# Loading and rounding a second weight piece ahead of x, and making the first scores in two halves, at the start of a fused attention and feed-forward kernel

## The chip, the cores and the metric

The kernel runs on one core of a Trainium2 chip. The metric is device time in microseconds (us) of that core. A run is one execution; most comparisons below rest on 5 runs of each kernel, taken in turn with runs of the kernel before on the same chip.

Names: TensorE multiplies matrices (PE in the profile, PEld for its weight loads), VectorE is DVE, ScalarE is ACT, SP issues the transfers.

## The reference, cut to what matters

```python
# x (8, 8, 512, 64), state (8, 8, 32, 64): batches, heads, tokens or states, width
scores = scale * x @ state.T           # softmax over the 32 states, for each token
xread  = softmax(scores) @ state
scores2 = scale * state @ x.T          # softmax over the 512 tokens, for each state
sread  = softmax(scores2) @ x
h = concat(xread, sread) @ w_in        # 4352 tokens x 512, w_in 512 x 2048
out = gelu_quick(h) @ w_out            # w_out 2048 x 512
```

The weights arrive as 64-bit floating-point words and are rounded to 32 bits on the chip, in pieces of 128 rows by 512 columns (512 KB each).

## The kernel before

It doesn't compute xread. It first multiplies the state by w_in (the product M) and then the softmax by M (h). So the first useful h matmul needs two things: four rounded pieces of w_in, from which M is made, and the normalised, transposed softmax of batch 0 (`aT`). All of this happens in the first 31 us, for which this is the code (comments are mine):

```python
def keep_warm(n):                         # warming: matmuls of zeros, 0.22 us each in the traces
    ps = psH.tile([P, FC], FP32, tag="h", name="warm")
    for _ in range(n):
        nc.tensor.matmul(ps, zeros[:, :P], zeros, start=True, stop=True)

def round_a(i):                           # a piece, first part: mask on VectorE, two passes on ScalarE
    ...
    nc.vector.tensor_scalar(sc, hi, 0x7FF00000, None, ALU.bitwise_and)
    ...
    nc.scalar.activation(out=sc.bitcast(FP32), in_=sc, func=AF.Relu, bias=edge[0], scale=-8.0)
    nc.scalar.activation(out=sc, in_=sc.bitcast(FP32), func=AF.Relu, bias=edge[1], scale=-1.0)

def round_b(i):                           # second part: four operations on VectorE
    nc.vector.tensor_scalar(fr, hi, 0xFFFFF, 0x100000, ...)
    nc.vector.scalar_tensor_tensor(sc, hi, -0x80000000, sc, ...)      # needs ScalarE's passes
    nc.vector.scalar_tensor_tensor(dst, lo, 2.0**-32, fr, ...)
    nc.vector.scalar_tensor_tensor(dst, dst, 2.0**-20, sc.bitcast(FP32), ...)

def att_xT_arriving(b, warm):             # x of batch 0, chunk by chunk as it lands
    for c in range(SCH):                  # 4 chunks of 128 tokens
        keep_warm(warm)
        ...                               # four transposes on TensorE
        (nc.scalar.copy if c % 2 else nc.vector.tensor_copy)(A[b]["xT"][...], ps)
...
load_weights(1); load_state(0); load_x(0); load_weights(NPR)     # NPR = 4
load_state(1); load_x(1); load_weights(2 * NPR)
keep_warm(11)
round_to(1, 0)          # piece 0
att_state(0)
att_xT_arriving(0, 2)
att_scores(0)           # all 512 tokens at once
powers_to(2)            # round_a of piece 1
att_blocks(0)           # transposes on VectorE
att_x_exp(0)            # maximum, subtraction, exponential
round_to(2, 1)
att_x_norm(0)           # sum, inverse, product, transpose: aT
keep_warm(24)
att_state(1)
...                     # transposes and scores of batch 1
keep_warm(24)
powers_to(4)
round_to(NPR, 2)        # pieces 2 and 3
att_M(0, 0)             # the first useful product, and its copy on ScalarE
att_blocks(1); att_x_exp(1)
up_x(0, 0) ...          # the first h
```

In the timelines the instructions of one engine stand in this order, and a wait stands with what ended it: VectorE's 1.34 us ahead of 6.91 us, for one, with ScalarE's pass.

## Time and profile before

| | |
|---|---|
| time, 3 runs | 747.86 us median (747.64 to 749.01) |
| span of the profiled run | 745.8 us |
| first M / first h on TensorE | 29.16 us / 31.00 us |
| fourth rounded piece ready on VectorE | 28.90 us |
| VectorE busy, 4.81 to 12.21 us | 4.04 of 7.40 us |
| VectorE busy, 12.21 to 28.90 us | 16.35 of 16.69 us |
| TensorE at half clock | 43.39 to 46.80 us |

TensorE is busy from here to the end (98% of the span), so what counts is when its first useful matmul starts, and whether it is held up or slowed after that. The lines are in the prediction.

### The profile page before, as it was taken

What the parts mean: (1) busy time and instruction counts of PE and PEld (TensorE: products, weight loads), DVE (VectorE), ACT (ScalarE), POOL (GpSimd) and SP (SyncE); (2) the same over time, 40 slices, a digit from 0 to 9 for tenths busy, and PEclk for the clock granted to TensorE, in tenths of its full rate; (3) what the DMA queues carried; (4) which work ended last, traced back from release to release, by engine and by line L of the source; (5) the groups of instructions that cost most, each with busy time, mean ns of one, the idle gap of its engine ahead of it and who ended that gap; (6) DMA issues with size and microseconds to landing.
All of it is one profiled execution on the core that took longest, in us unless ns stands there. A gap on an engine that the chain in (4) does not pass through costs nothing.

```text
span 745.8 us, 10913 instructions
## 1 busy us (share of the span) xinstructions
PE 732.2 (98%) x4553; PEld 568.0 (76%) x4555; DVE 501.9 (67%) x947; ACT 231.6 (31%) x421; POOL 0.8 (0%) x8
## 2 busy tenths in 40 slices
PE   8989999999999999999999999999999999999996
PEld 3423444458788798888888789878888888899995
DVE  5999699705946776576756765677657774768340
ACT  4667610121424411443134421451143313300220
POOL 0000000000000000000000000000000000000000
PEclk9999999999999999999999999999999999999999
DMA  9811246010012000300040003100030001000000
GB/s 234 337 58 56 85 142 173 0 54 3 29 46 45 1 15 30 74 1 15 2 102 1 15 2 83 21 1 16 29 74 1 15 2 42 1 15 29 15 1 28
DMA packets 48768, 35.29 MB, mean 47 GB/s; under 512 B 36432, under 2 KB 44112, under 8 KB 48720
## 3 DMA queue, kind: packets, MB, share of 16 engines
q1 hardware_dynamic: 48720, 34.61, 16.2%
q8 instruction: 35, 0.57, 0.3%
q14 instruction: 13, 0.11, 0.0%
HBM read 25.69 MB, written 8.91 MB: 46 GB/s over the span
## 4 chain that ended last, share of the span: by engine, by line
PE 95%; SPq 2%; DMA 1%; ACT 1%; issue 0%; DVE 0%; DVEq 0%; ACTq 0%
PE o L646 28%; PE o L891 16%; PE o L523 9%; PE h L462 8%; PE o L480 7%; PE low L598 6%; PE upx L891 6%; PE o L598 4%; PE M L280 4%; PE xT L262 2%; SPq L138 1%; PE sr L411 1%; PE o L280 1%; PE upx_sr L891 1%; DMA out_dram<-osb_sr 1%; PE warm L122 1%
## 5 line engine op out<-in xcount | busy, mean ns | idle before, releaser
L901 DVE TENSOR_TENSOR g<-o,g 128x512 f32<-128x512 f32 (+1 forms) x140 | 88.1, 651 | 87.4 <-PE o L891 86.3
L646 PE MATMUL o<-w_out,g 128*128 128x256 f32 x576 | 130.0, 380 | 0.0
L646 PEld LDWEIGHTS o<-w_out,g 128*128 128x128 f32 x576 | 107.4, 190 | 18.1 <-issue 4.2
L898 ACT ACTIVATE g<-g 128x512 f32<-128x512 f32 (+1 forms) x84 | 49.8, 599 | 100.5 <-DVE g L901 100.5
L891 PE MATMUL upx<-aT,M 128*128 128x256 f32 x192 | 49.3, 379 | 0.0
L891 PE MATMUL o<-ta,M 128*128 128x256 f32 x192 | 49.3, 379 | 0.0
L891 PE MATMUL o<-ta,ms 128*128 128x256 f32 x192 | 48.4, 380 | 0.0
L391 ACT COPY M<-M 128x512 f32<-128x512 f32 x64 | 33.2, 596 | 42.3 <-PE M L280 42.3
L646 PE MATMUL o<-sums,g 128*128 128x256 f32 x192 | 43.8, 382 | 0.0
L523 PE MATMUL o<-w_out,g 128*128 128x256 f32 x192 | 42.9, 380 | 0.0
L646 PE MATMUL o<-sums,later 128*128 128x256 f32 x192 | 42.4, 379 | 0.0
L646 PEld LDWEIGHTS o<-sums,g 128*128 128x128 f32 x192 | 35.6, 190 | 8.6 <-issue 4.2
L523 PEld LDWEIGHTS o<-w_out,g 128*128 128x128 f32 x192 | 36.1, 190 | 6.0 <-issue 1.3
L891 PEld LDWEIGHTS o<-ta,ms 128*128 128x128 f32 x192 | 36.4, 190 | 5.2 <-DVE osb L542 0.3
L891 PEld LDWEIGHTS upx<-aT,M 128*128 128x128 f32 x192 | 36.5, 190 | 5.0
L646 PEld LDWEIGHTS o<-sums,later 128*128 128x128 f32 x192 | 36.5, 190 | 5.0
L891 PEld LDWEIGHTS o<-ta,M 128*128 128x128 f32 x192 | 36.5, 190 | 5.0
L503 DVE TENSOR_TENSOR later<-g,g 128x512 f32<-128x512 f32 (+1 forms) x32 | 20.8, 650 | 21.5 <-ACT g L465 21.5
L462 PE MATMUL h<-low,M 128*128 128x512 f32 x64 | 31.5, 630 | 2.1 <-ACT M L391 2.1
L280 PE MATMUL M<-w_in,stT 64*32 64x512 f32 x512 | 33.2, 594 | 0.2 <-ACT eT L401 0.2
L462 PE MATMUL h<-aT,M 128*128 128x512 f32 x64 | 28.7, 599 | 2.3 <-ACT M L391 2.3
L601 DVE TENSOR_TENSOR pu<-low,pu 128x128 f32<-128x128 f32 x12 | 3.5, 291 | 39.6 <-PE low L598 39.6
(172 smaller groups left out, 1135.5 us busy)
## 6 DMA issues: line engine op xcount, KB each, us to landing
later<-in_moe_w_out_dram SPq DMA_DIRECT2D x16, 512.0 KB
xn<-in_x_dram SPq DMA_DIRECT2D x28, 256.0 KB
w_out<-in_moe_w_in_dram SPq DMA_DIRECT2D x12, 512.0 KB
out_dram<-osb SPq DMA_DIRECT2D x20, 256.0 KB
out_dram<-later SPq DMA_DIRECT2D x12, 256.0 KB
later<-in_moe_w_in_dram SPq DMA_DIRECT2D x4, 512.0 KB
sums<-in_x_dram SPq DMA_DIRECT2D x4, 256.0 KB
stn<-in_state_dram SPq DMA_DIRECT2D x16, 32.0 KB
```

The source lines that it names most:

```text
L262: nc.tensor.transpose(ps[:, c], x_heads(b, c, j), ident)
L280: nc.tensor.matmul(ps[g][st], A[b]["stT"][rows, st], rhs(rows, j), start=True, stop=True)
L391: nc.scalar.copy(m[:, g], ps[g])
L462: nc.tensor.matmul(hps, lhs[i], rhs[i], start=(i == 0), stop=(i == n - 1))
L480: nc.tensor.matmul(ops, G[key, f // 2][:, f % 2, P * r : P * (r + 1)], w_out[:, f], start=(f == 0), stop=(f == NF - 1))
L503: nc.vector.tensor_tensor(out=s1, in0=a21, in1=a22, op=ALU.add)
L523: nc.tensor.matmul(ps[:, r], lhs[f][:, P * r : P * (r + 1)], rhs[:, f], start=(first and r == 0 and f == 0), stop=(f == HF - 1), skip_grou ...
L598: nc.tensor.matmul(ps, lhs[f], rhs[:, f], start=(f == 0), stop=(f == QF - 1))
L646: nc.tensor.matmul(ps[:, r], lhs[f][:, P * r : P * (r + 1)], rhs[:, f], start=(r == 0 and f == 0), stop=(f == HF - 1), skip_group_check=True,)
L891: nc.tensor.matmul(ps[:, k], lhs[i][:, o : o + P], rhs[i], start=(first and k == 0 and i == 0), stop=(i == n - 1), skip_group_check=True,)
L898: nc.scalar.activation(out=dst, in_=src, func=AF.Gelu_apprx_sigmoid)
L901: nc.vector.tensor_tensor(out=dst, in0=ps, in1=x, op=ALU.add)
```

## The change

The intent is to use the time in which VectorE waits. The second piece of w_in is loaded ahead of x and rounded while x is still on its way; and the first softmax is begun on the first 256 tokens as soon as these are there. To pay for the late x, all four copies of transposed x go to ScalarE, and fewer warming matmuls stand in front of M. The diff, cut to its core:

```diff
-    def round_a(i):
+    def mask(i):
         ...                                  # the mask alone, so that it can be issued early
+    def round_a(i):
+        if i not in power:
+            mask(i)
@@ att_xT_arriving
-            keep_warm(warm)
+            if c < 2:
+                keep_warm(warm)
 ...
-            (nc.scalar.copy if c % 2 else nc.vector.tensor_copy)(A[b]["xT"][...], ps)
+            nc.scalar.copy(A[b]["xT"][...], ps)
+            if c % 2:
+                att_half(b, c // 2)
+    def att_half(b, i):                      # scores of 256 tokens, their transposes,
+        ...                                  # maximum and subtraction
@@ the start
-    load_weights(1)
+    load_weights(2)
 ...
-    keep_warm(11)
-    round_to(1, 0)
+    keep_warm(16)
+    powers_to(2)
+    round_to(2, 0)
     att_state(0)
     att_xT_arriving(0, 2)
+    nc.scalar.activation(out=A[0]["e1"], in_=A[0]["e1"], func=AF.Exp, scale=scale)
     att_scores(0)
     powers_to(2)
-    att_blocks(0)
-    att_x_exp(0)
-    round_to(2, 1)
+    round_to(3, 0)
     att_x_norm(0)
 ...
     att_scores(1)
-    keep_warm(24)
+    keep_warm(14)
     powers_to(4)
     round_to(NPR, 2)
     att_M(0, 0)
```

The whole scores of batch 0 are still made, because the other softmax needs them. Behind the first M the lists of instructions are the same on every engine.

## The prediction

> **What bounds the kernel now.** I read the page first: matmuls fill the core, and the chain that ended last is almost all TensorE.

> ```profile
> PE 732.2 (98%) x4553; PEld 568.0 (76%) x4555; DVE 501.9 (67%) x947; ACT 231.6 (31%) x421; POOL 0.8 (0%) x8
> PE 95%; SPq 2%; DMA 1%; ACT 1%; issue 0%; DVE 0%; DVEq 0%; ACTq 0%
> ```

> Behind such a queue a saving counts only if real TensorE work starts sooner or an idle time of TensorE goes. "Busy" includes the warming matmuls, which compute nothing, so I next read the chain in order of time over the first 50 us (columns: start, length, what).

> ```profile
> 24.32 4.91 PE warm L122 x22
> 29.23 1.15 PE M L280 x16
> 30.39 0.57 ACT M L391
> 31.00 7.15 PE h L462 x16
> ...
> 41.51 0.48 ACT M L391
> ...
> 42.03 8.84 PE h L462 x16
> ```

> The useful stream starts with the first product M, at 29.16 us in the timeline; from there to the end TensorE hardly rests. So the change is worth what it takes off 29.16. M needs two things: the end of the warming queue, and four rounded pieces of w_in from VectorE. The timeline of VectorE shows that both come nearly together.

> ```profile
> 4.81 0.43 DVE L189 TENSOR_SCALAR low<-w_out 128x512 int32<-128x512 int32 x1 [3.68 <-DMA w_out<-in_moe_w_in_dram]
> ...
> 6.91 0.69 DVE L205 SCALAR_TENSOR_TENSOR low<-w_out,low 128x512 int32<-128x512 int32 x1 [1.34 <-ACT low L195]
> ...
> 9.95 0.69 DVE L273 COPY xT<-xT 128x512 f32<-128x512 f32 x1 [0.42 <-PE xT L272]
> 12.21 0.43 DVE L189 TENSOR_SCALAR low<-w_out 128x512 int32<-128x512 int32 x1 [1.56 <-DMA w_out<-in_moe_w_in_dram]
> ...
> 28.21 0.69 DVE L207 SCALAR_TENSOR_TENSOR w_in<-w_in,low 128x512 f32<-128x512 f32 x1
> ```

> The fourth piece is done at 28.90, 0.26 us before M. From 12.21 VectorE has no named wait; before that it waits 3.3 us in three places. Thus VectorE is the real bound of the start, and the 24 warming matmuls in front of M only fill its time. A table of stretches confirms this and shows one more thing, the clock.

> ```profile
> core 0: us, PE busy (x) PEld busy (x) DVE busy (x) ACT busy (x) POOL busy (x), PEclk, DMA share, GB/s
> 4.81:12.21 7.40, 6.17 (x44) 2.83 (x42) 4.04 (x8) 2.77 (x5) 0.00 (x0) 1.00 1.11 284
> 12.21:28.90 16.69, 16.21 (x95) 7.67 (x89) 16.35 (x27) 10.57 (x16) 0.00 (x0) 1.00 1.03 331
> 43.39:46.80 3.41, 3.41 (x5) 1.35 (x4) 3.34 (x7) 1.93 (x3) 0.00 (x0) 0.50 0.00 0
> ```

> VectorE is busy 4.04 of 7.40 us in the first stretch and 16.35 of 16.69 in the second. In the last one, TensorE ran at half clock for 3.41 us although it was fully busy: half of that, 1.7 us, is lost on the bounding engine (16 h matmuls took 8.84 us instead of 7.15).

> [...] the half-clock stretch is 3.41 us, and just before it TensorE idles 2.12 us (39.91 to 42.03) waiting for the copy of M. [...] that window, 39.97 to 43.39, still had about 40% of work. [...] 5.0 to 8.5 us, where all packets are under 512 B (x), moved 237 GB/s; stretches of weights alone, from 24 us on, move about 400.

> **The change, part by part.** The order of instructions on each engine, which the built kernel shows, differs in the start alone; behind the first M all engines have the same lists.

> *Transfers.* The second piece (512 KB) goes ahead of x. At 400 GB/s it lands 1.3 us behind the first, at an estimated 6.1 us instead of 12.2, and x arrives up to 1.3 us later. Bytes up to the third piece are the same, so all else arrives as before.

> *VectorE.* Mask of piece 0 at 4.81; mask of piece 1 at 6.1, inside the wait for ScalarE that ends at 6.91 as before; the remaining three operations of piece 0 until 8.85; four of piece 1, 0.34+0.60+0.72+0.69 = 2.35 us by their spacing in the timeline, until 11.2. The first half of the scores should be there: chunk 1 of x, transposed at 7.96 before, comes about 9.0-9.2; its copy on ScalarE (0.59) ends near 10.3; the half scores take an estimated 0.6 (1.09 for whole ones); 11.0. Each half costs VectorE two transposes of 256 columns (estimate from 655 ns at 512 and 1245 at 1024: 0.36 each), a maximum and a subtraction of 512 (0.69 each): 2.1 us, so 13.2. The second half of x, copied by ScalarE one chunk after the other, gives scores about 13.4, so VectorE ends the second half at 15.4. Then a new wait: the third piece is masked only now, and ScalarE does the exponential (1.06) first and its two passes for the piece (0.72 each) after it: they end about 17.9, while VectorE has only 0.75 us of its own. I put the wait at 1.8 us. Three operations (2.0): 19.9. Normalising as before (1.24+0.22+0.38+1.26+1.2 = 4.3): 24.2. Three masks and one mask of the fraction (1.4), a wait of 0.45 for ScalarE's passes on the fourth piece, three operations (2.05): 28.15.

> As a ledger: gone are the waits of 0.42 and 1.56 and two copies of 0.69, 3.36 us; new are waits of about 0.2, 1.8 and 0.45 and 0.2 for the smaller operations, 2.65. VectorE gains about 0.7 us, 28.90 to 28.2.

> *TensorE.* Whole scores of batch 0 are still made for the other softmax, so 16 matmuls of half width are added twice, about 1.1 us, all in the start. Warming matmuls go from 11+8+24+8+24 = 75 to 16+4+24+8+14 = 66. From the second half scores (12.7): 0.6 for these, 1.02 for the whole scores, 24 warming matmuls at 0.216 (5.2): 19.5; four transposed groups at 0.87 with 0.1 ahead (3.6) 23.1, x of batch 1 has long landed; scores of batch 1 as before, 1.8 from the last transpose: 24.9; 14 warming matmuls and the small gap 3.3: 28.2. The shorter warming queue was evidently cut to meet VectorE at the same moment.

> *Sum.* M starts at 28.2-28.3 instead of 29.16: 0.9 us. Everything behind it keeps its order. ScalarE ends its passes for pieces 4 and 5 at about 29.0, and M's product needs it at 29.4, so the 0.9 survives; the idle time before 42.03 moves along with it, because it consists of ScalarE's queue behind the last gelu (four passes, two copies).

> **The rivals.** (1) *The half-clock window.* [...] the same 2.12 us of idle may be split between two windows and the 1.7 us loss goes. With the phase of the recorded run, the idle would lie at 39.0 to 41.1, about 1.0 and 1.1 us in two windows, neither half idle: 745.2 us. For it: the shift alone would do it. Against it: the phase may be new in every run; then the chance of a loss is the same before and after. All three times of before and the profiled run are 747.6 or more, so the loss seems common there. (2) *New waits eat the gain*: x or the copies, now all on ScalarE, arrive a microsecond later than I put them, the second half and the exponential follow, and M starts at 29.2 again: 747.8. For it: four copies in series on one engine and a late x. Against it: the warming queue of 14 suggests an earlier M. (3) *The start loses its clock.* With no warming between the later chunks TensorE may idle enough to be halved; the 24 warming matmuls then take up to 1.7 us more and M slips: 748.5. For it: over a microsecond of waits lies between 9 and 13 us. Against it: windows there were 80% busy before and no loss came.

> **Range and chances.** 747.86 - 0.9 = 746.9 with the half-clock loss in the middle run; 745.2 without. I weigh these about three to two and take a little off for the second: 746.4. The range is 744.9 (both gains, and 0.3 more) to 747.9 (no gain). 2% is 15 us, while the whole start before M is 29 us and its bound moves by one: within 2% 0.99, faster 0.01, slower 0.

> **What would show it.** In the profile of the changed kernel: the first M near 28.2, VectorE's fourth piece ending just before it, a wait of about 1.8 us of VectorE for ScalarE's pass near 16-18 us, no wait for the second piece, scores half done near 11.0. The clock of 39 to 47 us tells whether the 1.7 us came back. I'm wrong if M starts at 28.2 and the time does not fall by 0.9 at an equal number of half-clock stretches, or if M waits for VectorE past 28.6.

## The result, and the profile after

The changed kernel took 745.72 us in the median of 4 runs (745.65 to 747.58), the kernel before 747.75 with one more run. Ratios here are the mean time of one kernel's runs over that of the other's of the same rounds, so not quite the ratio of the quoted medians: it was 0.9978, with a 95% interval of 0.9956 to 1.0. The time lies in the predicted range and below the predicted 746.4. But the four runs are three at 745.65 to 745.77 and one at 747.58, and nothing in between.

The page of the changed kernel, first the engines, then the chain:

```profile
PE 730.2 (98%) x4576; PEld 567.4 (76%) x4578; DVE 501.1 (67%) x949; ACT 232.7 (31%) x423; POOL 0.8 (0%) x8
PE 96%; DMA 2%; ACT 1%; SPq 0%; issue 0%; DVE 0%; DVEq 0%; ACTq 0%
```

TensorE was busy 2.0 us less, 730.2 instead of 732.2, although it has 23 more matmuls. Something took less time for each matmul. The chain in order of time (start, length, what) shows where it went:

```profile
25.88 2.75 PE warm L122 x12
28.63 1.55 PE M L289 x16
30.18 0.57 ACT M L415
...
30.80 7.15 PE h L486 x16
...
41.30 0.48 ACT M L415
...
41.82 7.15 PE h L486 x16
```

The first h starts at 30.80; before, it was 31.00. This is all that the start has won: 0.2 us, where I had reckoned 0.9. The second group of 16 h starts 0.2 us earlier as well, at 41.82, but takes 7.15 us where before it took 8.84. That is the other 1.7 us. The table of stretches has the clock (columns as in the prediction; the sixth after the length, the number ahead of the DMA share, is the granted clock):

```profile
4.81:12.21 7.40, 6.31 (x43) 2.95 (x42) 5.79 (x12) 4.14 (x7) 0.00 (x0) 1.00 1.04 251
12.21:28.90 16.69, 15.86 (x120) 7.57 (x125) 13.79 (x24) 9.43 (x15) 0.00 (x0) 1.00 0.99 308
37.53:40.95 3.42, 2.17 (x17) 0.31 (x16) 3.39 (x5) 2.92 (x5) 0.00 (x0) 1.00 0.00 0
40.95:44.36 3.41, 2.54 (x6) 1.25 (x7) 3.34 (x7) 1.82 (x5) 0.00 (x0) 1.00 0.03 7
```

VectorE does 1.75 us more in the first stretch (5.79 against 4.04), as intended, and 2.56 us less in the second (13.79 against 16.35): it got its early work and then stood still for longer. The last two lines are two windows of 3.41 us, the length of the halved stretch of before, counted from the recorded start of full clock at 6.81 us. TensorE's idle time, 39.70 to 41.82, is just as long as before, but in this run it lies across the two. Busy shares are 0.64 and 0.74 and the clock stays whole. In the profiled run of before, one window took nearly all of it, with a share of 1.36/3.42 = 0.40, and the next was halved:

```profile
39.97:43.39 3.42, 1.36 (x3) 0.68 (x4) 3.35 (x8) 2.46 (x5) 0.00 (x0) 1.00 0.01 2
```

VectorE's timeline shows why the start won so little (in brackets idle time and what ended it; the second operation of a rounding is L211 here, L205 before, and L301 is the transpose of a half):

```profile
6.33 0.43 DVE L189 TENSOR_SCALAR low<-w_out 128x512 int32<-128x512 int32 x1 [1.10 <-DMA w_out<-in_moe_w_in_dram]
...
11.72 0.78 DVE L301 STREAM_TRANSPOSE e<-sh 128x256 f32<-128x256 f32 x2 [0.43 <-PE sh L289]
...
14.14 0.78 DVE L301 STREAM_TRANSPOSE e<-o 128x256 f32<-128x256 f32 x2 [0.19 <-PE o L289]
...
18.86 0.69 DVE L211 SCALAR_TENSOR_TENSOR low<-w_out,low 128x512 int32<-128x512 int32 x1 [1.82 <-ACT low L201]
...
27.00 0.69 DVE L211 SCALAR_TENSOR_TENSOR low<-w_out,low 128x512 int32<-128x512 int32 x1 [0.54 <-ACT low L201]
...
28.33 0.69 DVE L213 SCALAR_TENSOR_TENSOR w_in<-w_in,low 128x512 f32<-128x512 f32 x1
```

The second piece was there at 6.33 instead of 12.21, as planned. The big new wait of 1.82 us is the one of the prediction (1.8). The fourth piece ends at 29.02: 0.12 us later than before, not 0.7 earlier.

So the 0.2 us at the first h do not come from VectorE. Before, the warming matmuls held M until 29.23 (chain), 0.33 us after the fourth piece (28.90), and the first h came 2.10 us after that piece. Now the queue, ten matmuls shorter, lets M begin at 28.63, its last part waits for the fourth piece, and the first h comes 1.78 us after the piece. No run shortens the queue of the kernel before alone; by these figures (an estimate, 28.90 + 1.78) its first h would come near 30.7, about as early as here.

So two things have to be tested: is the 2 us really the clock, and so luck of the run? And what did each part of the change do to the start?

### The profile page after: what moved, and what is told of

It reads as the page before. It is cut to its first block, busy times and chain, and to the rows that moved or that the text cites. A ratio compares the mean times of both kernels' runs of the same rounds, so it can differ in the third digit from the quotient of the medians.

```text
span 744.0 us, 10961 instructions
## 1 busy us (share of the span) xinstructions
PE 730.2 (98%) x4576; PEld 567.4 (76%) x4578; DVE 501.1 (67%) x949; ACT 232.7 (31%) x423; POOL 0.8 (0%) x8
## 3 DMA queue, kind: packets, MB, share of 16 engines
q1 hardware_dynamic: 48720, 34.61, 16.3%
## 4 chain that ended last, share of the span: by engine, by line
PE 96%; DMA 2%; ACT 1%; SPq 0%; issue 0%; DVE 0%; DVEq 0%; ACTq 0%
PE o L670 28%; PE o L915 16%; PE o L547 9%; PE h L486 8%; PE o L504 7%; PE low L622 6%; PE upx L915 6%; PE o L622 4%; PE M L289 4%; PE xT L268 2%; PE warm L122 1%; PE o L289 1%; PE sr L435 1%; PE upx_sr L915 1%; DMA out_dram<-osb_sr 1%; PE eT L424 1%
## 5 line engine op out<-in xcount | busy, mean ns | idle before, releaser
L527 DVE TENSOR_TENSOR later<-g,g 128x512 f32<-128x512 f32 (+1 forms) x32 | 20.8, 650 | 23.1 <-ACT g L489 23.1
L486 PE MATMUL h<-low,M 128*128 128x512 f32 x64 | 29.8, 600 | 2.1 <-ACT M L415 2.1
L486 PE MATMUL h<-aT,M 128*128 128x512 f32 x64 | 28.7, 599 | 2.2 <-ACT M L415 2.2
```

The lines of the kernel that those rows point to most:

```text
L486: nc.tensor.matmul(hps, lhs[i], rhs[i], start=(i == 0), stop=(i == n - 1))
L527: nc.vector.tensor_tensor(out=s1, in0=a21, in1=a22, op=ALU.add)
```

## The experiments

"Filled" below means one added line, 8 warming matmuls (1.73 us) where TensorE waits for the second M:

```diff
     att_M(1, 0)
+    keep_warm(8)
     ...
     turn(1, 0, None, [1, 1])
```

### The clock: both kernels filled

**Before, filled (b_fill).** 

> The kernel before, with 8 warming matmuls (1.73 us) between the second product M and the h matmuls that wait for its copy: TensorE's idle of 2.12 us at 39.9 to 42.0 us is filled, nothing else moves. Theory A (nearly all of the measured 2 us is the stretch of half clock that follows this idle in some runs): every run at 745.8 to 746.2, no half-clock stretch inside the span, h matmuls 7.15 us instead of 8.84. Theory B (the change's earlier start earns the 2 us, the clock is a side matter): it stays near 747.7. Theory C (filling delays the h matmuls): 748 to 749.

Measured: 746.03 us median, 745.82 to 746.34 in all 5 runs (one of them above the expected 746.2). The kernel before, in 11 runs, spread from 745.73 to 748.30, with 747.64 in the median. In the profile the filled stretch is followed by h at full clock (chain in order of time):

```profile
31.06 7.15 PE h L462 x16
...
42.08 7.15 PE h L462 x16
```

**After, filled (a_fill).** 

> The changed kernel with the same 8 warming matmuls. Theory A: 745.5 to 745.8 in every run, that is 0.2 us under the filled kernel before, since the first h matmul starts at 30.80 instead of 31.00; the one run in four at 747.6 no longer occurs. Theory B: 745.7 as well, but 2 us under the filled kernel before.

Measured: 745.67 us median, 745.58 to 746.03 in 5 runs (two above the expected 745.8), the mean 0.30 us under that of the filled kernel before, though the ranges overlap. Theory A holds. Eight matmuls of zeros, which add no time (the second group of h starts 11.02 us after the first, before 11.03), do for the kernel before what the change seemed to do: its median falls by 1.6 us. Between the two kernels there remain 0.3 us. In the profiles the fourth piece ends at 28.93 and 28.87, the first h starts at 31.06 and 30.65: of these 0.41 us VectorE gives 0.06, and the rest is, by these traces, again the shorter warming queue.

### The changed kernel again, twice

No edit.

**a_again.** 

> The changed kernel itself, again, to see how often its clock is halved. Theory A1 ([...] the idle of 2.12 us is the same in both kernels): about as often as before, that is in 6 or 7 of 11 runs at 747.2 to 747.7 and the others at 745.6 to 745.9; the first four runs were luck and the true difference of the medians is only 0.3 us. Theory A2 (the idle lies better in the window, since the phase is tied to the start): almost all runs at 745.7.

**a_again2.** 

> The same once more, for the share of runs with a half-clock stretch: A1 in about 60% of the runs, A2 in at most one of five.

Measured: 747.02 to 747.44 in all 5 runs of the first; 745.60, 745.67, 746.89, 747.33, 747.54 and 747.62 in the 6 of the second. The kernel before, in 11 runs beside them: 745.95 to 748.96. The ratios are 0.9996 (0.9984 to 1.0008) and 0.9989 (0.9974 to 1.0003). Taken together, the changed kernel had 9 of 15 runs at 747.0 or more (60%, median 747.27) and the kernel before 28 of 46 (61%, median 747.56). The line at 747.0 is a rough sign: at least four of the 28 had a whole granted clock (0.998 or more). By a granted clock of 0.997 or less it is 9 of 15, and 21 of the 42 runs of before that have their clock on record. Theory A1 holds: nothing shows that the change makes the loss rarer, and the first four runs were luck. In the profiled run of a_again the half clock is back, behind a window with a busy share of 1.29/3.41 = 0.38 (table of stretches):

```profile
38.90:42.31 3.41, 1.29 (x16) 0.34 (x3) 3.38 (x6) 3.20 (x6) 0.00 (x0) 1.00 0.00 0
42.31:45.73 3.42, 3.42 (x6) 1.36 (x5) 3.32 (x8) 0.72 (x2) 0.00 (x0) 0.50 0.03 7
```

The run at 746.89 is of a third kind. It was profiled, and its clock was whole. Here the second piece was masked at 7.56 instead of 6.33, so all of the start was 1.2 us late. The medians are thus mixtures, and only the filled kernels compare cleanly.

### The early load alone (b_load_fill)

The filled kernel before, with one line changed:

```diff
-    load_weights(1)
+    load_weights(2)
     load_state(0)
```

> The filled kernel before with one part of the change alone: the second piece is loaded ahead of x, nothing is rounded earlier. If the later x sets VectorE's chain (x chunks land 1.2 to 1.7 us later in the trace of the changed kernel), the first h starts at about 32.2 instead of 31.0 and the time is 1.0 to 1.5 us over the filled kernel before. If x had slack, the wait of 1.56 us for the second piece goes and it is up to 0.5 us faster.

Measured: 748.23 us median (747.95 to 748.40), 2.2 us over the filled kernel before, more than expected. The first h starts at 33.25. VectorE now waits 2.35 us for the third chunk of x to be transposed and then again for the scores, which before cost it nothing (timeline; the transposes of the scores began at 12.67 before):

```profile
12.59 0.69 DVE L273 COPY xT<-xT 128x512 f32<-128x512 f32 x1 [2.35 <-PE xT L272]
...
15.28 1.31 DVE L293 STREAM_TRANSPOSE e<-o 128x512 f32<-128x512 f32 x2 [1.66 <-PE o L280]
```

There is a second part. With x late and only 11 warming matmuls ahead of it, TensorE stood still at 5.6 to 7.4 us; the window from 5.09 to 8.50 was 40% busy, and the transposes from 8.50 to 11.91 ran at half clock. How the 2.2 us divide between late x and slow transposes I haven't separated. The next experiment gives a hint: with the same loads and no half clock there, its whole scores begin at 13.07, here at 14.10, and in the profile of before at 11.49; so about 1.0 of the 2.6 us may be the clock (it also differs in copies and warming matmuls). The early load is a price, and the rest of the change has to earn it back. The five more warming matmuls at the very start of the changed kernel seem to have a purpose too; no run tests them alone.

### The change without the halves (a_whole_fill)

```diff
-            if c % 2:
-                att_half(b, c // 2)
 ...
-    nc.scalar.activation(out=A[0]["e1"], in_=A[0]["e1"], func=AF.Exp, scale=scale)
     att_scores(0)
-    powers_to(2)
+    att_blocks(0)
+    att_x_exp(0)
```

> The filled changed kernel without the halves: scores, transposes, maximum and subtraction of batch 0 once over all tokens, behind the last chunk of x; early load and early rounding stay. If the halves matter because VectorE would otherwise stand still from 11.3 us until whole scores are there at about 14.1, the subtraction ends at 17.9 instead of 16.3 and the time is 1.2 to 1.7 us over the filled changed kernel. If x late is all that counts and the halves only cost extra instructions, equal within 0.3.

Measured: 748.76 us median, 747.50 to 750.30 in 6 runs. VectorE stands still from the end of the second piece until whole scores are there (timeline):

```profile
14.25 1.31 DVE L315 STREAM_TRANSPOSE e<-o 128x512 f32<-128x512 f32 x2 [2.85 <-PE o L287]
```

The subtraction ends at 18.09 instead of 16.36, 1.7 us later. The two fastest runs, 747.50 and 747.71, are 1.8 to 2.0 us over the filled changed kernel, just past what I expected. The slower ones have a new stretch of half clock: M waited for VectorE until 30.79, and the profiled run was halved from 32.16 to 35.57 (its first 16 h took 8.64 us instead of 7.13), where the fill of this experiment doesn't reach. So the halves are worth some 1.8 us, most of the 2.2 us that the early load alone cost.

### The third piece masked earlier (a_mask_fill)

The 1.82 us come from an order: the third piece is masked behind the second half, so ScalarE does the exponential first. Here the mask stands ahead of the second half's maximum, and 8 warming matmuls fewer stand before M:

```diff
             nc.vector.transpose(a["e1"][:, g, w]..., ps[g])
+        if i == 1:
+            powers_to(3)
 ...
-    keep_warm(14)
+    keep_warm(6)
```

> The filled changed kernel with the mask of the third piece moved ahead of the second half's maximum, so that ScalarE does its two passes before the exponential, and 8 warming matmuls fewer before M. If the new wait of 1.82 us of VectorE is what holds the first product back, it goes, the fourth piece is done at 27.2 instead of 29.0 and the time is 1.6 to 1.9 us under the filled changed kernel: 743.8 to 744.1. If the transfers or ScalarE's queue hold it, under 0.5 us.

Measured: 744.41 us median (744.28 to 744.46), 1.26 us under the filled changed kernel: the direction is right, the size 0.3 us short. The fourth piece ends at 27.60, in the filled changed kernel at 28.87: these 1.27 us are the whole gain, and the shorter warming queue only lets it through. The wait is gone, the next one grew:

```profile
23.74 0.43 DVE L189 TENSOR_SCALAR low<-w_out 128x512 int32<-128x512 int32 x1 [0.24 <-DMA w_out<-in_moe_w_in_dram]
...
25.58 0.69 DVE L211 SCALAR_TENSOR_TENSOR low<-w_out,low 128x512 int32<-128x512 int32 x1 [1.07 <-ACT low L201]
```

Because VectorE is earlier, the passes for the fourth piece queue on ScalarE behind the copies of batch 1, and the mask of a later piece meets its transfer. Instead of 1.82 + 0.54 us VectorE waits 0.24 + 1.07. The first h starts at 29.37.

### All four pieces ahead of the normalisation (a_best)

The first h needs M, which needs four pieces and then about 2 us of TensorE and ScalarE, and it needs the normalised softmax, 4.3 us of VectorE. Rounding first and normalising last puts these side by side. The edit also masks the fourth piece ahead of the third one's remaining operations, since `round_to(3, 0)` goes and `powers_to(4)` takes its place:

```diff
+        if i == 1:
+            powers_to(3)           # as above
 ...
-    round_to(3, 0)
-    att_x_norm(0); keep_warm(24); att_state(1)
+    powers_to(4); round_to(NPR, 0)
+    att_x_norm(0); keep_warm(20); att_state(1)
     for j in range(NPR):
-        keep_warm(2)
         att_xT(1, j)
-    att_scores(1); keep_warm(14); powers_to(4); round_to(NPR, 2)
     att_M(0, 0)
+    att_scores(1); powers_to(NPR + 2); keep_warm(5)
 ...
     att_M(1, 0)
+    keep_warm(12)
```

> Also from this: third and fourth piece both rounded ahead of the normalisation of batch 0, M made ahead of the scores of batch 1, no warming between the transposes of batch 1, 12 filling matmuls later. VectorE loses the waits of 1.82 and 0.54 us and the copy of M on ScalarE lies beside the normalisation, so the first h starts at about 26.1 instead of 30.65. Part is given back: the h of batch 1 waits for VectorE's chain (37.9 instead of 41.7) and the next M for piece 8 (about 45.9 instead of 48.7). Expected 742.7 to 743.2; if the chain of batch 1 on VectorE gives back more, 743.8 or more.

Measured: 742.21 us median (742.12 to 742.40), 0.5 us under what I expected, ratio to the kernel before 0.9928 (0.9916 to 0.9940), outputs correct. From 12.21 to 25.65 us VectorE is busy 12.94 of 13.44 us, and what the first h waits for last is the softmax (timeline):

```profile
25.87 7.11 PE L488 MATMUL h<-aT,M 128*128 128x512 f32 x16 [0.21 <-DVE aT L369]
```

The first h starts 4.8 us earlier than in the filled changed kernel; 3.5 us of it reach the end, since the h of batch 1, at 38.24, wait for a chain of their own: maximum and subtraction of batch 1 on VectorE, exponential (1.06 us), table load (1.28) and gelu on ScalarE, then M, then the 12 filling matmuls. The first copy of M ended at about 37.8, so these twelve may cost some 0.5 us here (an estimate; a shorter filling was not tried).

### What belongs to the reordering, and what to the change

**The kernel before with the reordering alone (b_order)**, 20 warming matmuls ahead of the transposes of batch 1, 16 behind its scores. 

> The kernel before with the order of the best version only, none of the change: four pieces rounded ahead of the normalisation of batch 0, M ahead of the scores of batch 1, 16 warming matmuls behind them and 12 later. If the reordering is what wins, VectorE's chain ends at 28.2 (its waits of 0.42 and 1.56 us at the start stay) and the first h starts there instead of 31.0: about 743.5 to 744.8. If the reordering pays only with the change, 745.5 or more.

**The changed kernel with the reordering, masks left late (a_order)**, 20 and 14. 

> The changed kernel with the same reordering but the third piece masked where the change has it, behind both halves. VectorE keeps the wait of 1.82 us and gets one of about 1.1 for the fourth piece, so its chain ends at 28.7: about 744.0 to 745.2, no better than the reordered kernel before. Against the best version (742.2, first h at 25.87) the difference is then the price of the late mask alone, 2 to 2.8 us; if it comes under 743.2, the late mask costs little and my account of the wait is wrong.

Measured: 745.75 us (745.37 to 746.42) and 746.78 us (745.87 to 748.63). These two were inconclusive, by my own fault. VectorE's chain ended near where expected, at 28.32 (28.2) and 29.07 (28.7), but ScalarE's passes now stood ahead of a copy that TensorE needs for batch 1, TensorE stood still (1.78 us in b_order, 2.56 in a_order), and its clock was halved. For b_order the table of stretches has it:

```profile
19.59:23.01 3.42, 1.59 (x12) 1.26 (x12) 3.39 (x7) 3.12 (x6) 0.00 (x0) 1.00 0.99 374
23.01:26.42 3.41, 3.41 (x27) 1.07 (x32) 3.27 (x6) 0.96 (x2) 0.00 (x0) 0.50 1.02 400
```

So the queue of warming matmuls ended late, and the first h started at 30.53. In the second try only their numbers differ:

```diff
-    keep_warm(20)
+    keep_warm(38)      # 35 in the changed kernel
 ...
-    keep_warm(16)
+    keep_warm(8)       # 14 to 5 in the changed kernel
```

**b_order2.** 

> The reordered kernel before with its warming mended: 38 warming matmuls ahead of the transposes of batch 1 instead of 20, so that TensorE doesn't stand still and get halved from 23.0 to 26.4 us while ScalarE works off its passes, and 8 instead of 16 behind the scores. VectorE's chain ended at 28.3 in the first try and should do so again; the first h follows at about 28.4 instead of 30.5. The next bound is VectorE's eighth piece at about 47.9, 1.2 us ahead of where the filled kernel before makes that M: 744.6 to 745.0.

**a_order2.** 

> The reordered changed kernel with the late mask, mended alike (35 and 5). VectorE's chain ended at 29.1 and its eighth piece comes about 48.8: 745.4 to 745.8, so 0.7 us or so slower than the reordered kernel before and 3.3 slower than the best version, which differs in the place of one mask. If it comes at 743 or less, the late mask isn't what costs.

Measured: 744.76 us (744.55 to 745.00) and 745.61 us (745.59 to 745.63), both as expected. In b_order2 the first h follows VectorE directly; in a_order2 VectorE waits at two pieces (one line of each timeline, of TensorE and of VectorE; the 1.82 us at the third piece come before the wait in the second line, as above):

```profile
28.53 7.11 PE L462 MATMUL h<-aT,M 128*128 128x512 f32 x16 [0.60 <-DVE aT L343]
```

```profile
22.76 0.69 DVE L211 SCALAR_TENSOR_TENSOR low<-w_out,low 128x512 int32<-128x512 int32 x1 [1.21 <-ACT low L201]
```

These medians tell the parts apart:

| kernel, clock kept up | median us |
|---|---|
| before, filled | 746.03 |
| before, reordered (b_order2) | 744.76 |
| after, filled | 745.67 |
| after, reordered, late masks (a_order2) | 745.61 |
| after, reordered, early masks (a_best) | 742.21 |

(a_best ran on another chip than the four above it; the kernel before had medians of 747.61 there and 747.64 and 746.89 here, mixtures of its two levels.)

My expectation speaks of one mask. The code shows two: a_best masks the third piece ahead of the second half's maximum, and the fourth ahead of the third one's remaining operations; a_order2 has both late, and each has its wait, 1.82 and 1.21 us. Reordering the changed kernel gives nothing (745.67 to 745.61) while the masks are late: the first h starts 1.45 us earlier (29.20 instead of 30.65), but the h of batch 1 hardly move (41.58 instead of 41.68). The two masks together are worth 745.61 - 742.21 = 3.4 us once the order is right, near to their two waits of 3.0 and to the 3.33 us by which the first h moves (29.20 to 25.87); the two kernels differ also in 35 or 20 warming matmuls, and what each mask is worth in this order wasn't tested. With its masks in place the change is worth 744.76 - 742.21 = 2.55 us over the reordered kernel before; with them late it is 0.85 worse.

## Why the prediction was right or wrong

The time, 745.72, lies in the range, but that it lies below 746.4 is luck: over all 15 runs the median is 747.27, still in the range. Point by point:

- **What bounds the start: right in part.** The first M is held by VectorE's fourth piece and the warming queue together, and most of what the start gains or loses here reaches the end: in the filled kernels the first h moves by 0.41 us (31.06 to 30.65) and the mean time by 0.30. But "VectorE is the real bound", with warming matmuls that "only fill its time", left out that the queue itself held M for the last 0.3 us; dropping this is nearly all of the 0.41, by the traces; no run tests it alone.
- **The second piece at an estimated 6.1 us: right** (6.33).
- **VectorE done with the fourth piece at 28.2: wrong**, it was 29.02. The failed step is "The first half of the scores should be there", with chunk 1 of x at "about 9.0-9.2" and the scores at 11.0. The chunk was transposed at 9.66, 1.70 us later than before where I allowed 1.3, and VectorE began at 11.72 after a wait of 0.43 (0.5 us off). The other term is the price of a half: I put its end 2.0 us on (11.2 to 13.2), and it took 2.2, since two short transposes took 0.78 instead of 0.72 and small gaps stand between the operations (maximum and subtraction took the 0.69 each that I had put); twice, 0.4 us. Together 0.9 us, which is what was missing. The early-load experiment shows from the other side that a late x is costly.
- **The new waits: right** in place and size, 1.82 for "1.8" and 0.54 for "0.45". Moving the mask removed the first, and in the reordered kernel the waits at the third and fourth piece proved to be the largest loss of all.
- **M at 28.2 to 28.3: half wrong.** The warming queue ended at 28.56, and M then took 1.56 us instead of 1.09, its last part waiting for the late fourth piece. I had written that M behind 28.6 waiting for VectorE would prove me wrong; its last part did.
- **"The 0.9 survives": wrong in size.** 0.2 us of first h in the profile, 0.3 us of time between filled kernels, and VectorE's part in it is at most 0.06.
- **Rival 1, the half-clock window: right in the split, which made the measured 2 us:** the same 2.12 us of idle lay across two windows, 0.64 and 0.74 busy, and the clock stayed whole, where a window 0.40 busy was followed by the half clock before. My saying that "the chance of a loss is the same before and after", if the phase is new in every run, was the true half of it: 60% of the runs against 50 to 61%, by the sign one takes. My saying that the shift alone would end the loss fell with a_again. My figure of 745.2 for the lucky case was 0.5 us under the measured one; the start gained 0.7 less than it assumed.
- **Rival 2, that late x and the copies eat the gain, came true for most of it**, and should have had the weight that I gave to the 0.9. **Rival 3** did not come in the changed kernel, whose profile has no halved window in the start, but it did in the early-load kernel and in two of the reordered ones.
- **The chances: right**; the ratio is within 2%.

## What to carry to other kernels

Where TensorE stood still for 2.12 us here, its clock was halved in some runs and not in others (in 9 of the changed kernel's 15, by the granted clock), and a change elsewhere can seem to win or lose by that; fill such an idle time in both kernels before comparing, or look at the granted clock and the single runs rather than at a median of four. Work moved ahead on one engine paid little here until its partner's work moved with it: moving one mask, so that ScalarE's passes come earlier, won 1.26 us, where the whole change had won 0.3. And where two things are needed at once, do first the one that has further steps on other engines behind it.
